# Sorted block attention with a max-out MoE: W2 turned by DMA transposes, and the loads of the later items reordered

## The chip, the cores and the metric

One core of a Trainium2 chip. The metric is the device time of one execution in microseconds; the kernel before takes 166.34 us (median of 3 runs, 166.28 to 167.09). The profile is of one execution with a span of 165.0 us. TensorE multiplies matrices, VectorE (DVE) and ScalarE (ACT) compute on rows and empty PSUM, GpSimd (POOL) issues the loads that cast from float32 to bfloat16, SyncE (SP) issues the stores and DMA transposes.

## The reference

```python
# q, k, v: (4, 8, 768, 64); sort_net: (4, 8, 8, 8); w1, w2: (512, 1024); w_out: (1024, 512)
P = sort_net
for _ in range(5):
    P = exp(P - max(P, -1)); P = P / sum(P, -1); P = P / sum(P, -2)
k_sorted = einsum('bhij,bhjcd->bhicd', P, k_b)     # 8 blocks of 96 rows, mixed by P
v_sorted = einsum('bhij,bhjcd->bhicd', P, v_b)
attn = softmax(q_b @ k_sb^T / 8)                   # within each block
x = (attn @ v_sb) as (3072 tokens, 512)            # heads beside each other
out = maximum(x @ w1, x @ w2) @ w_out              # float32
```

## The kernel before

The batch has four items (b = 0 to 3), each of 8 heads and 768 tokens. For each item the kernel sorts keys and values (a product of the blocks with a block-diagonal matrix made from P), turns queries and keys so that the head dimension lies on partitions, computes scores and their exponentials, the products with the values, a normalisation by a column of ones, and transposes the result x into `xT`. Then comes the MoE for its tokens.

The maximum is rewritten: max(x w1, x w2) w_out = relu(x (w1 - w2)) w_out + x (w2 w_out). So the kernel forms w1 - w2 in place (`w_difference`, in four column quarters; two on GpSimd, two on VectorE, called diff2 and diff3), and once the product wc = w2 w_out (`w_product`, four row blocks). That product needs W2 with its columns on partitions, `w2T`. `w2_transposes` (L634) makes it with TensorE: 16 transposes of 128 x 128 into a PSUM tile, twice, each tile emptied by VectorE or ScalarE. W2 arrives in three column parts, and each group needs the columns up to its own.

The order of all work is written by hand; every engine runs its own instructions in program order. Three pieces set it:

- `front`, a list of names for item 0: k, v (sorts), tq (query transposes), SC (scores), VA (values and normalisation), tx (x transposes), tw (W2 transposes), h..a and h..b (halves of an MoE product of w1 - w2 with xT; h13 is token half 1, column quarter 3), diff, pe2 (block diagonals of the other items), F (512 columns of filler products on TensorE). A last A or D says whether ScalarE or VectorE evacuates.
- For each item b a list of units: 8 `moe_h` (none for b = 0, whose are in `front`), for b = 0 the four `w_product`, then 12 half `moe_out`. So for b = 0 the units 0 to 7 are empty, 8 to 11 are the products for wc, 12 to 23 the outputs.
- `first_tail`, `second_tail`, `third_tail`: the steps of the next item's attention that are put after each unit: KS (key sorts), TQ and `q_transposes`, TURN (`turn_v`, VectorE, which reorders the raw values), VS (value sorts), SC, VA, TR (`x_transposes`, DMA transposes issued by SyncE for items 1 to 3), `pair_q` (copies that set two heads side by side, for the DMA transposes of queries of items 2 and 3).

`evac` (L102) chooses ScalarE or VectorE by a running estimate of their loads (`pick`), unless told. PSUM has four buffers of two banks (`ps_f32`, `ps_bf16`), shared by all products; an unread buffer holds up TensorE.

Loads are issued by GpSimd and wait in its queue, in program order, for the buffer that they overwrite and, when many are in flight, for an older load. The copies into `seen` (L771, L822) are there for order alone: GpSimd waits in them for what they read, and with it the loads behind them. Item 0's values, keys and queries come first, then the parts of W1 and W2, w_out, item 1's keys, item 1's queries, the values of items 1 and 2, item 2's keys and queries (queries of item 2 go into the space of W2, once it is used up). Item 3's values follow in the tail of item 0; its keys and queries go into the space of its own raw values (`load_k`, `load_q`), so they wait until those are turned, in unit 12 of `second_tail`.

Of the kernel before, what the change touches and what calls it, by code (L numbers as in the profile page):

```python
# [11 lines left out]
BF16 = mybir.dt.bfloat16  # L12
# [4 lines left out]
def kernel(  # L17
# [16 lines left out]
    nc = tc.nc  # L34
# [4 lines left out]
    B, H, S, D = q.shape  # L39
# [7 lines left out]
    R = S // 128  # L47
    PB = 128 // NB
    HP = H // 2
# [19 lines left out]
    def ps_bf16(name):  # L69
        return psum.tile([128, 2048], BF16, tag="ps", name=name)  # L70
# [32 lines left out]
    def evac(out_ap, in_ap, n, two_x=False, eng=None):  # L103
        a_ns, d_ns = (200 + n) / 1.2, (130 + (n / 2 if two_x else n)) / 0.96
        if eng:
            load[eng] += a_ns if eng == "A" else d_ns
        if (eng or pick(a_ns, d_ns)) == "A":
            nc.scalar.copy(out=out_ap, in_=in_ap)  # L108
        else:
            nc.vector.tensor_copy(out=out_ap, in_=in_ap)  # L110
# [21 lines left out]
    def load_q(b, by_pair=False):  # L132
        if b == 2:
            t = w2_sb.rearrange("p t f -> p (t f)")[:, 0 : H * R * D].rearrange(
                "p (h x) -> p h x", h=H
            )
        elif b == 3:
            t = v_raw[:, HB * D :].rearrange("p (h x) -> p h x", h=H)
        else:
            t = qpool.tile([128, H, R * D], BF16, tag="q_raw", name="q_raw", bufs=1)  # L140
        src = q[b].rearrange("h (p r) d -> p h (r d)", r=R)
        for hs in [slice(hp, H, HP) for hp in range(HP)] if by_pair else [slice(0, H)]:
            nc.gpsimd.dma_start(out=t[:, hs], in_=src[:, hs])
        q_raw[b] = t
# [5 lines left out]
    NCH = 3  # L150

    def load_k(b):
        k_raw[b] = (
            kpool.tile([128, HB * D], BF16, tag="k_raw", name="k_raw")
            if b < 3
            else v_raw[:, 0 : HB * D]
        )
        n = HB * D // NCH
        for ci in range(NCH):
            nc.gpsimd.dma_start(  # L160
                out=k_raw[b][:, ci * n : (ci + 1) * n],
                in_=k_src[b, :, ci * n : (ci + 1) * n],
            )

    def load_v(b, pieces=2, which=None, half=None):
        r0 = (b % 2 if half is None else half) * 64
        n = BLK * D // pieces
        for m in range(pieces) if which is None else [which]:
            nc.gpsimd.dma_start(  # L169
                out=v_raw[r0 : r0 + 64, m * n : (m + 1) * n],  # L170
                in_=v_src[b, :, m * n : (m + 1) * n],
            )

    w1_sb = big.tile([128, HP, DFF], BF16, tag="w1", name="w1_sb")
    w2_sb = big.tile([128, HP, DFF], BF16, tag="w2", name="w2_sb")
# [10 lines left out]
    def load_w_columns(dst, src, t0, t1):  # L186
        s = src.rearrange("(t p) f -> p t f", p=128)
        c = slice(t0 * DFF // 4, t1 * DFF // 4)
        nc.gpsimd.dma_start(out=dst[:, :, c], in_=s[:, :, c])  # L189
# [208 lines left out]
    nc.vector.memset(v_sb[:, :, D : D + 1], 1.0)  # L398
    xT = big.tile([128, 2, 2, 2, 2, TCH], BF16, tag="xT", name="xT")

    q_pair = {}

    def pair_q(b, two):

# [226 lines left out]
    w2T = big.tile([128, NFB, DMODEL], BF16, tag="w2T", name="w2T")  # L631
    wc = big.tile([128, HP, DMODEL], BF16, tag="wc", name="wc")

    def w2_transposes(t, eng):  # L634
        ps = ps_bf16("tw_ps")
        for n in range(16):
            fb, dmt = t * 4 + n // 4, n % 4
            nc.tensor.matmul(  # L638
                ps[:, n * 128 : (n + 1) * 128],
                w2_sb[:, dmt, fb * 128 : (fb + 1) * 128],  # L640
                ident,
                is_transpose=True,
                start=True,
                stop=True,
            )
        return lambda: evac(
            w2T[:, t * 4 : t * 4 + 4, :].rearrange("p f d -> p (f d)"),
            ps,
            2048,
            two_x=True,  # L650
            eng=eng,
        )

    def w_product(dmt):
# [59 lines left out]
    def moe_out(b, ti, part):  # L714
        slot = ti % 2
        if slot == 0 and part == 0:
            out_ps[0] = ps_f32("out_ps")
        ps = out_ps[0]
        out_products(ps[:, slot * 512 : (slot + 1) * 512], b, ti, part=part)
        if slot == 1 and part == 1:  # L720
            tok0 = b * S + ti * 128
            o = opool.tile([128, 2, 512], FP32, tag="o", name="o")
            evac(o.rearrange("p t n -> p (t n)"), ps, 1024)
            nc.sync.dma_start(
                out=out[tok0 - 128 : tok0 + 128, :].rearrange("(t p) n -> p t n", p=128),
                in_=o,
            )
# [34 lines left out]
    for c, n, m in [(2, 2, 0), (4, 3, 1)]:  # L762
# [4 lines left out]
    turn_v(first, "A", 36, 56)  # L767
    turn_v(first, "A", 56, 80)
    block_diagonals_first()
    seen = const.tile([128, 2, 2], BF16, tag="seen", name="seen")  # L770
    nc.gpsimd.tensor_copy(out=seen[0:G, 0], in_=p_bf[:, NB - 1, NB - 2 :])  # L771
    load_w_columns(w2_sb, moe_w2, 0, 1)
    selections(1)
# [1 line left out]
    turn_v(first, "D", 80, 96)  # L775

    front = """
        k0A k1D k2A v1A v2D v0A tq0D F0 v3D SC1 SC0 tq1D
        SC4 F2 VA1 SC5 F1 VA0 SC3 SC2 VA4 tx0D SC7 F3
        VA3 VA2 SC6 tw0D h00a tx1A tw1A VA5 diff3 diff2 h01a h00bA  # L780
        h01bA tx2A h03a VA6 h03bA VA7 h02a h13a tx3D h02bD h12a h13bA
        pe2 h12bD h10a h11a h10bA h11bA
    """.split()
    fills = [0]

    def fills_due():
# [3 lines left out]
    def front_step(step):  # L790

        eng = step[-1] if step[-1] in "AD" else None
        name = step[:-1] if eng else step
        kind = name.rstrip("0123456789ab")
        n = [int(x) for x in name if x.isdigit()]
        if kind == "F":
            fills[0] = 512
        elif kind == "k":
            sort_k(0, n[0], 640 if step == front[0] else 0, eng)
        elif kind == "v":  # L800
            sort_v(0, n[0], 0, eng)
        elif kind == "tq":
            q_transposes(0, n[0], eng)
        elif kind == "SC":
            scores(0, n[0], fills_due())
        elif kind == "VA":
            values(0, n[0], fills_due())
        elif kind == "tx":
            x_transposes(0, n[0], eng)
        elif kind == "tw":  # L810
            w2_transposes(n[0], eng)()
        elif kind == "diff":
            w_difference(n[0])
        elif kind == "pe":
            block_diagonals([(0, 2), (0, 3), (1, 1), (1, 2), (1, 3)], 2)
        elif name[-1] == "a":
            moe_h_products(0, n[0], n[1], (0, 2), fills_due())
        else:
            moe_h(0, n[0], n[1], eng, (1, 3))

    front_step(front[0])
    nc.gpsimd.tensor_copy(out=seen[:, 1], in_=kT[0][:, 0:2])  # L822
    load_w_columns(w1_sb, moe_w1, 0, 1)
    load_w_columns(w2_sb, moe_w2, 1, 2)
    selections(3)
    load_w_columns(w1_sb, moe_w1, 1, 2)
    load_w_columns(w2_sb, moe_w2, 2, 4)
    load_w_columns(w1_sb, moe_w1, 2, 4)
    load_w(wo_sb, moe_w_out)
    w_difference(0, nc.gpsimd)  # L830
    w_difference(1, nc.gpsimd)
    load_k(1)
    for step in front[1:-26]:
        front_step(step)

    load_q(1)
    for piece in range(2):
        for b in (1, 2):
            load_v(b, which=piece)
    load_k(2)  # L840

    for step in front[-26:]:
        front_step(step)
# [7 lines left out]
    def sorts_and_scores(b):  # L851
# [6 lines left out]
    TURN = [lambda c=c: turn(both, c) for c in (0, 24, 48, 72)]  # L858
    first_tail = {
        7: KS,  # L860
        9: [TQ[0], TURN[0]],
        10: [SC[0], TQ[1], TURN[1]],
        11: SC[1:4] + TURN[2:4] + [lambda half=half: load_v(3, half=half) for half in range(2)],
        12: VS[0:3],
        13: VS[3:6],
        14: VS[6:8] + [SC[4]],
        15: [VA[0], lambda: pair_q(2, 0)],
        16: [VA[1], lambda: pair_q(2, 1)],
        17: SC[5:8] + [TR[0]],
        18: [VA[2]],  # L870
        19: [VA[3], TR[1]],
        20: [VA[4]],
        21: [VA[5], TR[2]],
        22: [VA[6], VA[7], TR[3]],
    }
    SC, VA, TR, KS = sorts_and_scores(2)
    VS = [lambda t=t: sort_v_halved(3, t) for t in range(4)]
    TURN = [lambda c=c: turn(both, c) for c in (0, 24, 48, 72)]
    second_tail = {
        0: [lambda: q_transposes(2, 0), lambda: q_transposes(2, 1)],  # L880
        2: KS,
        4: SC[0:2],
        5: [VA[0]],
        6: SC[2:4] + [TURN[0]],
        7: [VA[1], TR[0]],
        8: [VA[2], TURN[1]],
        9: [VA[3], TR[1], TURN[2]],
        10: SC[4:7],
        11: [VA[4], TURN[3]],
        12: [VA[5], TR[2], lambda: load_k(3), lambda: load_q(3)],  # L890
        13: [VA[6]],
        14: SC[7:8] + VS[0:2],
        15: [VA[7], TR[3]],
        16: VS[2:4],
        17: [lambda: pair_q(3, 0)],
        18: [lambda: pair_q(3, 1)],
    }
    SC, VA, TR, KS = sorts_and_scores(3)
    third_tail = {
        0: [lambda: q_transposes(3, 0), lambda: q_transposes(3, 1)],  # L900
        2: KS,
        5: SC[0:2],
        6: [VA[0]],
        7: [VA[1], TR[0]],
        8: SC[2:5],
        9: [VA[2]],
        10: [VA[3], TR[1]],
        11: [VA[4]],
        12: SC[5:8],
        13: [VA[5], TR[2]],  # L910
        14: [VA[6]],
        16: [VA[7], TR[3]],
    }
    tails = [first_tail, second_tail, third_tail, {}]
    for b in range(B):
# [52 lines left out]
```

The softmax here doesn't subtract the row's maximum and nothing guards it: scores larger than these inputs give would overflow.

## Time and profile before

| | us |
|---|---|
| time, median of 3 | 166.34 |
| span of the profiled execution | 165.0 |
| TensorE busy | 157.0 |
| VectorE busy | 77.5 |
| ScalarE busy | 82.3 |
| GpSimd busy | 33.9 |
| W2 transposes on TensorE | 2 groups of 1.07 |
| their evacuations | DVE 1.21, ACT 1.87 |

The page gives busy time and number of instructions of each engine, the busy share in 40 slices of the span, and the chain of work that ended last: followed back from the last instruction, at each step to what released it, or to the instruction before it on its engine. A timeline row gives start, duration, engine, line, operation, output<-inputs, shapes, how many were merged, and in brackets the idle time before it and what ended it. A load's landing is dated by who was released by it.

### The profile page before, as it was taken

The page shows a single profiled execution, that of the slowest core. Times are in us where ns is not written, and L with a number is a line of the kernel's source. Part 1 is how long each engine was busy: PE and PEld are TensorE (multiplying, and loading weights), DVE is VectorE, ACT ScalarE, POOL GpSimd, SP SyncE. Part 2 cuts the span into 40 slices and gives each one's busy share as a digit, 9 for nine tenths or more (in the row PEclk, how much of TensorE's full clock was granted, in tenths as well). Part 3 has the DMA queues.
Part 4 walks back from the last instruction along what each step waited for, and adds up shares of the span by engine and source line. Part 5 has one row for each costly group of instructions (what it writes and reads, how often), then busy time and mean ns, then how long its engine had stood idle before and what let it go on. Part 6 is the DMA issues. An engine that isn't in the chain of part 4 may idle for free.

```text
span 165.0 us, 4561 instructions
## 1 busy us (share of the span) xinstructions
PE 157.0 (95%) x2007; PEld 95.4 (58%) x2025; DVE 77.5 (47%) x170; ACT 82.3 (50%) x101; POOL 33.9 (21%) x61
## 2 busy tenths in 40 slices
PE   7889999999999999999999999999999999999992
PEld 7839776756554555557655554575655546654451
DVE  4878995684366564525277763250642420000011
ACT  3489776617239846055652353457447206642020
POOL 7949997131206000000014010000000000000000
PEclk9999999999999999999999999999999999999999
DMA  3999999999999999689515999995025294000333
GB/s 41 204 204 194 164 196 207 209 205 220 210 203 204 220 224 167 175 84 228 111 19 104 126 212 157 200 309 29 0 52 175 50 164 142 0 0 0 127 131 127
DMA packets 30404, 23.90 MB, mean 145 GB/s; under 512 B 16752, under 2 KB 25200, under 8 KB 30384
## 3 DMA queue, kind: packets, MB, share of 16 engines
q0 software_dynamic: 11040, 13.37, 50.0%
q1 hardware_dynamic: 19200, 10.17, 28.9%
q8 instruction: 16, 0.26, 0.7%
q10 hardware_dynamic: 144, 0.07, 0.1%
q14 instruction: 4, 0.03, 0.1%
HBM read 26.75 MB, written 6.29 MB: 200 GB/s over the span
## 4 chain that ended last, share of the span: by engine, by line
PE 81%; DMA 6%; DVE 5%; ACT 3%; POOL 2%; issue 2%
PE out_ps L704 37%; PE h_ps L677 25%; DMA w_sb<-in_moe_w_dram 5%; PE wc_ps L657 4%; PE o_ps L575 4%; PE k_ps L458 3%; PE s_ps L548 3%; ACT e L556 1%; POOL w_sb L189 1%; PE v_ps L523 1%; DMA p_sb<-in_sort_net_dram 1%; PE tq_ps L433 1%; DVE colsum L276 1%; DVE p_sb L273 1%; PE tw_ps L638 1%
## 5 line engine op out<-in xcount | busy, mean ns | idle before, releaser
L704 PE MATMUL out_ps<-wo_sb,g 128*128 128x512 bf16 (+2 forms) x187 | 46.0, 370 | 1.4 <-issue 1.0
L677 PE MATMUL h_ps<-xT,w_sb 128*128 128x384 bf16 x256 | 44.5, 326 | 0.0
L677 PEld LDWEIGHTS <-w_sb 128*128 128x128 bf16 x256 | 24.0, 98 | 15.5
L556 ACT ACTIVATE e<-s_ps 96x768 bf16<-96x768 f32 x32 | 24.0, 805 | 14.8 <-PE s_ps L548 14.8
L691 ACT ACTIVATE g<-h_ps 128x768 bf16<-128x768 f32 x27 | 21.7, 811 | 17.4 <-PE h_ps L677 17.3
L704 PEld LDWEIGHTS <-g 128*128 128x128 bf16 x200 | 17.1, 97 | 15.8
L704 PE MATMUL out_ps<-wc,xT 128*128 128x512 bf16 (+2 forms) x98 | 24.7, 370 | 0.1
L108 ACT COPY o<-out_ps 128x1024 f32<-128x1024 f32 x10 | 10.1, 1012 | 28.0 <-PE out_ps L704 25.2
L592 DVE TENSOR_TENSOR x<-o_ps,rs 96x512 bf16<-96x512 f32 x32 | 22.0, 687 | 1.1
L704 PEld LDWEIGHTS <-xT 128*128 128x128 bf16 x100 | 9.6, 97 | 11.2
L575 PEld LDWEIGHTS <-e 96*128 96x128 bf16 x256 | 11.7, 97 | 5.7 <-DVE v_sb L110 0.2
L586 DVE RECIPROCAL rs<-o_ps 96x8 f32<-96x8 f32 x32 | 6.4, 201 | 17.2 <-PE o_ps L575 17.1
L739 DVE COPY o<-out_ps 128x512 f32<-128x512 f32 (+1 forms) x2 | 1.2, 625 | 27.6 <-PE out_ps L704 27.6
L575 PE MATMUL o_ps<-v_sb,e 96*128 96x65 bf16 x256 | 12.7, 193 | 0.0
L110 DVE CAST kT<-k_ps 128x1024 bf16<-128x1024 f32 x6 | 7.2, 1222 | 8.4 <-PE k_ps L458 8.4
L110 DVE CAST v_sb<-v_ps 96x1024 bf16<-96x1024 f32 x7 | 8.5, 1219 | 4.9 <-PE v_ps L523 2.2
L160 POOL DMA_DIRECT2D v_raw<-in_k_dram x3 | 2.5, 838 | 35.1 <-DVE v_dc L250 31.4
L108 ACT CAST v_sb<-v_ps 96x1024 bf16<-96x1024 f32 x9 | 8.8, 1015 | 1.6 <-PE v_ps L500 0.8
L169 POOL DMA_DIRECT2D v_raw<-in_v_dram x11 | 6.5, 593 | 12.7 <-DVE v_dc L250 6.4
L693 DVE TENSOR_SCALAR g<-h_ps 128x768 bf16<-128x768 f32 x5 | 4.8, 957 | 8.9 <-PE h_ps L677 8.8
L548 PEld LDWEIGHTS <-kT 64*128 64x128 bf16 x256 | 6.1, 94 | 4.8 <-issue 2.6
L548 PE MATMUL s_ps<-qT,kT 64*128 64x96 bf16 x256 | 8.5, 204 | 0.3 <-DVE qT L110 0.2
(97 smaller groups left out, 144.4 us busy)
## 6 DMA issues: line engine op xcount, KB each, us to landing
out_dram<-o SPq DMA_DIRECT2D x11, 512.0 KB, 3.4
v_raw<-in_v_dram POOLq DMA_DIRECT2D x8, 384.0 KB, 13.5
k_raw<-in_k_dram POOLq DMA_DIRECT2D x9, 256.0 KB, 11.0
w_sb<-in_moe_w_dram POOLq DMA_DIRECT2D x4, 256.0 KB, 6.0
w_sb<-in_moe_w_dram POOLq DMA_DIRECT2D x2, 512.0 KB, 9.6
wo_sb<-in_moe_w_out_dram POOLq DMA_DIRECT2D x2, 512.0 KB, 13.7
v_raw<-in_v_dram POOLq DMA_DIRECT2D x3, 256.0 KB, 5.0
q_raw<-in_q_dram POOLq DMA_DIRECT2D x4, 192.0 KB, 9.1
```

Source lines behind the costliest of these rows:

```text
L108: nc.scalar.copy(out=out_ap, in_=in_ap)
L110: nc.vector.tensor_copy(out=out_ap, in_=in_ap)
L169: nc.gpsimd.dma_start(out=v_raw[r0 : r0 + 64, m * n : (m + 1) * n], in_=v_src[b, :, m * n : (m + 1) * n],)
L548: nc.tensor.matmul(ps[:, h2 * 512 + ii * 128 : h2 * 512 + ii * 128 + BLK], kT[b][rows, (hp * 8 + i) * BLK : (hp * 8 + i) * BLK + 128], rhs ...
L556: nc.scalar.activation(out=e[:, 0 : 8 * BLK].rearrange("p (t c r) -> p t c r", t=8, r=R), in_=ps[0:BLK] .rearrange("p (t f) -> p t f", t=8 ...
L575: nc.tensor.matmul(ps[:, h2 * 512 + ii * 65 : h2 * 512 + (ii + 1) * 65], e[:, (h2 * 4 + ii) * BLK : (h2 * 4 + ii) * BLK + 128], v_sb[:, m0 ...
L586: nc.vector.reciprocal(out=rs, in_=ov[:, :, :, 64])
L592: nc.vector.tensor_tensor(out=x, in0=ov[:, :, :, 0:D], in1=rs.to_broadcast([BLK, 2, 4, D]), op=ALU.mult,)
L657: nc.tensor.matmul(ps[:, 0:512], w2T[:, fb, dmt * 128 : (dmt + 1) * 128], wo_sb[:, fb, :], start=(fb == 0), stop=(fb == NFB - 1),)
L677: nc.tensor.matmul(h_ps[ch, t][:, m * 512 : m * 512 + TCH], w1_sb[:, hp, fb * 128 : (fb + 1) * 128], xT[:, b % 2, ch, hp % 2, hp // 2, :], ...
L691: nc.scalar.activation(out=g, in_=src, func=AF.Relu)
L704: nc.tensor.matmul(dst, g_tiles[b, ch, m // 2][:, m % 2, off : off + 128] if m < NFB else xT[:, b % 2, ch, hp % 2, hp // 2, off : off + 12 ...
```

## The change

- `w2_transposes` no longer uses TensorE: SyncE issues four DMA transposes, one for each 128 rows of W2, straight into `w2T`. They stand behind all loads of W2. The column loads are reordered, so that the last of W2 is now the last of the six weight parts.
- A third `seen` copy, from the columns of `w2T` that the second transpose writes, stands on GpSimd between item 1's keys and all later loads, so that these start only when that transpose has landed. Item 1's queries are loaded in four parts and the values of items 1 and 2 in eight.
- `front` has a new order: scores, values and h products of item 0 come in another sequence, the W2 transposes are gone, and the fills are added up instead of replaced.
- Item 2's keys are loaded late, in the tail of item 0. Item 3's values are loaded in interleaved halves, its keys and queries get buffers of their own and are loaded right behind its values, after a wait (`hold_loads`) for item 2's query transposes.
- In the tails nearly all steps move: of item 1 the query transposes go from units 9 and 10 to 12 and 13, the turns of the values from 9 to 11 to units 14 and 15, value sorts from 12 to 14 to 17 to 19, x transposes from 17 to 22 to 21 to 23. The tails of items 2 and 3 move by about one unit.
- The output evacuations of item 1 are fixed on ScalarE. The normalisations of the attention stay on VectorE in both kernels.

It is meant to take the transposes and their evacuations off TensorE, VectorE and ScalarE, and to keep later loads out of the way of the DMA transposes.

```diff
@@ load_q, load_k
-        elif b == 3:
-            t = v_raw[:, HB * D :].rearrange("p (h x) -> p h x", h=H)
...
-        k_raw[b] = (
-            kpool.tile([128, HB * D], BF16, tag="k_raw", name="k_raw")
-            if b < 3
-            else v_raw[:, 0 : HB * D]
-        )
+        k_raw[b] = kpool.tile([128, HB * D], BF16, tag="k_raw", name="k_raw")
@@ new
+    seen = const.tile([128, 3, 2], BF16, tag="seen", name="seen")
+    def hold_loads(b):
+        nc.gpsimd.tensor_copy(out=seen[:, 0], in_=qT[b][:, HP - 1, R - 1, 126:128])
@@ w2_transposes
-    def w2_transposes(t, eng):
-        ps = ps_bf16("tw_ps")
-        for n in range(16):
...
-        return lambda: evac(
...
+    def w2_transposes(dmt):
+        nc.sync.dma_start_transpose(
+            out=w2T[:, :, dmt * 128 : (dmt + 1) * 128],
+            in_=w2_sb[:, dmt, :],
         )
@@ moe_out
-            evac(o.rearrange("p t n -> p (t n)"), ps, 1024)
+            evac(o.rearrange("p t n -> p (t n)"), ps, 1024, eng="A" if b == 1 else None)
@@ front
-        k0A k1D k2A v1A v2D v0A tq0D F0 v3D SC1 SC0 tq1D
-        SC4 F2 VA1 SC5 F1 VA0 SC3 SC2 VA4 tx0D SC7 F3
-        VA3 VA2 SC6 tw0D h00a tx1A tw1A VA5 diff3 diff2 h01a h00bA
-        h01bA tx2A h03a VA6 h03bA VA7 h02a h13a tx3D h02bD h12a h13bA
-        pe2 h12bD h10a h11a h10bA h11bA
+        k1A k0A v1D k2A v2A v0D tq0D v3A tq1D SC4 SC5 F2
+        F3 VA4 SC6 SC7 VA5 F0 SC0 VA6 SC1 VA7 F1 SC3
+        tx2D SC2 tx3D VA1 h10a VA0 VA2 h10bA h11a tx0A h11bA diff3
+        VA3 diff2 h13a h01a tx1D h03a h13bD h03bD h01bA h12a pe2 h00a
+        h02a h00bD h02bA h12bA
@@ loads
     load_w_columns(w1_sb, moe_w1, 0, 1)
     load_w_columns(w2_sb, moe_w2, 1, 2)
+    load_w_columns(w1_sb, moe_w1, 1, 2)
+    load_w_columns(w1_sb, moe_w1, 2, 4)
+    load_w_columns(w2_sb, moe_w2, 2, 4)
+    load_w(wo_sb, moe_w_out)
     selections(3)
-    load_w_columns(w1_sb, moe_w1, 1, 2)
-    load_w_columns(w2_sb, moe_w2, 2, 4)
-    load_w_columns(w1_sb, moe_w1, 2, 4)
-    load_w(wo_sb, moe_w_out)
+    for dmt in range(HP):
+        w2_transposes(dmt)
     w_difference(0, nc.gpsimd)
     w_difference(1, nc.gpsimd)
     load_k(1)
+    nc.gpsimd.tensor_copy(out=seen[:, 2], in_=w2T[:, NFB - 1, 254:256])
...
-    load_q(1)
-    for piece in range(2):
+    load_q(1, True)
+    for piece in range(4):
         for b in (1, 2):
-            load_v(b, which=piece)
-    load_k(2)
+            load_v(b, 4, which=piece)
@@ first_tail (item 1)
-        9: [TQ[0], TURN[0]],
-        10: [SC[0], TQ[1], TURN[1]],
-        11: SC[1:4] + TURN[2:4] + [lambda half=half: load_v(3, half=half) for half in range(2)],
-        12: VS[0:3],
...
-        17: SC[5:8] + [TR[0]],
-        18: [VA[2]],
-        19: [VA[3], TR[1]],
-        20: [VA[4]],
-        21: [VA[5], TR[2]],
-        22: [VA[6], VA[7], TR[3]],
+        12: [TQ[0]],
+        13: [SC[0], TQ[1]],
+        14: SC[1:4] + TURN[0:2],
+        15: [SC[4]] + TURN[2:4] + [lambda: load_v(3, half=0), lambda: load_k(2)],
+        16: SC[5:7],
+        17: VS[0:3],
+        18: VS[3:6],
+        19: VS[6:8],
+        20: [VA[0], SC[7], VA[1]],
+        21: [TR[0], VA[2], VA[3], TR[1]],
+        22: [VA[4], VA[5], TR[2]],
+        23: [VA[6], VA[7], TR[3]],
@@ second_tail (item 2)
-        0: [lambda: q_transposes(2, 0), lambda: q_transposes(2, 1)],
+        0: [lambda: pair_q(2, 0), lambda: pair_q(2, 1)],
+        1: [
+            lambda: q_transposes(2, 0),
+            lambda: q_transposes(2, 1),
+            lambda: hold_loads(2),
+            lambda: load_v(3, half=1),
+            lambda: load_q(3),
+            lambda: load_k(3),
+        ],
         2: KS,
...
-        12: [VA[5], TR[2], lambda: load_k(3), lambda: load_q(3)],
```

## The prediction

> **What bounds the kernel now.** I read the page's busy line and slices first, then the chain of waits in order of time, then the timeline of 11 to 52 us, then windows of single stretches.
>
> ```profile
> PE 157.0 (95%) x2007; PEld 95.4 (58%) x2025; DVE 77.5 (47%) x170; ACT 82.3 (50%) x101; POOL 33.9 (21%) x61
> ...
> DMA  3999999999999999689515999995025294000333
> ```
>
> TensorE is busy for 157.0 of 165.0 us, and the transfers are saturated for the first 16 slices, 66 us. So two things run at their limit side by side in the first part of the kernel: whatever leaves TensorE there is worth something only as far as the data are there earlier too. The chain shows where each of them sets the pace:
>
> ```profile
> 16.36 0.67 POOL w_sb L189
> 17.03 8.72 DMA w_sb<-in_moe_w_dram
> 25.75 0.05 issue
> 25.80 1.07 PE tw_ps L638 x16
> ...
> 35.04 3.36 PE h_ps L677 x20
> 38.40 1.64 PE k_ps L458 x96
> 40.03 0.32 PE wc_ps L657
> ```
>
> Until 25.75 the weight loads set the end, and from 25.80 on TensorE itself, without a gap worth a microsecond. The second batch of W2 transposes (tw_ps) stands at the hand-over. The timeline gives the landing times that matter here:
>
> ```profile
> 28.39 1.29 DVE L231 TENSOR_TENSOR w_sb<-w_sb 128x1024 bf16<-128x1024 bf16 x2 [0.32 <-DMA w_sb<-in_moe_w_dram]
> ...
> 34.19 0.52 POOL L169 DMA_DIRECT2D v_raw<-in_v_dram  x1 [1.91 <-DMA wo_sb<-in_moe_w_out_dram]
> ...
> 36.52 0.54 POOL L160 DMA_DIRECT2D k_raw<-in_k_dram  x1 [0.74 <-DMA k_raw<-in_k_dram]
> 37.75 0.53 POOL L160 DMA_DIRECT2D k_raw<-in_k_dram  x1 [0.70 <-DMA k_raw<-in_k_dram]
> 38.33 1.59 PEld L458 LDWEIGHTS <-k_raw 64*64 64x64 bf16 x96 [0.32 <-issue]
> ```
>
> GpSimd's queue waits for an older transfer before it issues a new one, so its releases date the landings: the last weight columns at 28.4, w_out at 34.2, the last third of item 1's keys at 37.7. TensorE sorts those keys from 38.33, only 0.6 us later. The keys have almost no slack.
>
> How loads fare beside DMA transposes is seen in two windows, the first loads alone, the second with x transposes among the key loads of item 3 (columns: window; its length; busy us and instructions of PE, PEld, DVE, ACT, POOL; clock; DMA share; GB/s):
>
> ```profile
> 31.00:35.00 4.00, 4.00 (x41) 2.46 (x38) 2.64 (x5) 0.97 (x2) 1.03 (x2) 1.00 1.15 210
> ...
> 91.00:95.00 4.00, 4.00 (x41) 2.19 (x39) 3.41 (x6) 1.00 (x2) 0.38 (x1) 1.00 1.39 119
> ```
>
> With a higher busy share the engines move little over half as much. That is the resource on which I rest the forecast.
>
> **What the skill says.** "DMA: Bandwidth & Descriptors", section "Queues, rings and completion order": each DMA engine goes round-robin between the queues with work, packet by packet. The packet records agree: beside key loads of 2048-byte pieces, some 90 transpose pieces of 256 bytes and 66 key pieces go out per us, where the keys alone make 94. The same page, "Latency and other measured facts", gives DMA transposes 261 GB/s, so 256 KB would take an estimated 1.0 us; an undisturbed x transpose here moves its 768 pieces in about 1.2 us, which is of that size. "TensorE: Matmul & The Clock Gate", "The HAM clock gate", says that an idle window of about 3.4 us halves TensorE's clock; no stall in this trace is that long (the longest wait is 1.2 us), so it isn't shown here.
>
> **The change part by part.**
>
> *W2 off TensorE.* 32 transposes go: two groups of 1.07 us, 2.14 us. Their two evacuations (DVE 1.21 us, ScalarE 1.87 us) go too; those engines are not the bound there, so I count only the 2.14 us.
>
> *What of it arrives at the key sort.* In the new order the products h13, h01, h03, h12, h00 and h02 stand after the differences diff3 and diff2, which need the last weight columns at 28.4. Both orders queue the same six weight loads, so that time stays. The attention work and h10, h11 before it come to about 14 us of TensorE time from 11.5, plus its small waits: TensorE would be through at 26.3 and stand until diff3 ends at 29.05 (28.4 + 0.65). After that 6 x 1.30 of h, 0.34 of x transposes and 0.25 of block diagonals are left, 8.4 us: the sort of item 1's keys could begin at 37.5 instead of 38.33. So of 2.14 us only 0.8 arrives, and the sort would end at 39.2 rather than 40.03.
>
> *Four DMA transposes beside the loads.* They wait for the last W2 columns, now the last of the six, at 28.4; a transpose starts about 0.9 us after its issue, so 29.3. Each moves 128 x 1024 values, 1024 pieces of 256 bytes. At that time half of w_out (2.4 us alone) and item 1's keys (4 us alone) are still queued on the other ring. Item 3's loads price this: the 256 key pieces from 91 us needed 5.6 us beside one x transpose where they need 2.7 alone (+2.9, some of it to an output store), and the query load from 97 needed 7.5 instead of 4.1; less 0.9 for an output store, +2.5. Both times there was a stretch of 1 to 1.5 us in which nothing finished. About 1000 transpose pieces fall beside w_out and the keys, 1.3 times an x transpose: +3.3 us. The low end is the transpose's own time, +1.2; the high end, with a stall more, +5. I take +3.3: the last third of the keys lands at 41.0, its part of the sort takes 0.55, and the sort ends at 41.6. That is 1.6 us **later** than before. The first product of W2 and w_out waits for the first transpose as well: its 1024 pieces are through at about 40.5 and land about 1 us later, 41.5, the same time by another way. The three others then run alone at 1.0 to 1.4 us each and land ahead of their products (1.9 us each).
>
> *The gate on GpSimd.* The new copy waits for the second transpose, about 43.5 to 44. Behind it on GpSimd's queue stand item 1's queries and the values of items 1 and 2, nothing else. Queries (4.1 us) then land at about 50, values (7.7 us) at about 59. Before, those were 43 and 50. The change has moved their use back: query transposes after units 12 and 13, which is 51 to 54 by the sums above (four products of 1.9, units of 1.3), value sorts after unit 17, about 60.5. The last turn on VectorE ends at about 60. That is hidden with 0.5 us to spare: cost 0, up to 1 us at the high end.
>
> *The seam from item 0's MoE to item 1's.* The second x transpose of item 1 moves from unit 19 to unit 21 of 24. Before, it was held by an output store and its pieces ended at 69.2 for a product that began at 71.1. Now: two value products end 0.5 us after unit 21; VectorE has four normalisations in a row (0.92 each) and ends 2.1 us after it; shortest time to landing 2.8 us, so 4.9. TensorE has units 22 and 23 and six value products until then, 4.1, and two h products (0.32) before it needs that tile: it waits 0.5 us, 1.5 with the usual 3.8 us to landing. I take 0.7.
>
> *The rest.* Item 2's keys loaded late, item 3's values, keys and queries loaded ahead into their own buffers, pair copies (0.55 us each) and query transposes one unit on, item 1's output evacuations on ScalarE: in the windows from 71 to 136 us TensorE is idle for only some 0.9 us, so they can give little; and keys at the sort of item 2 come some 15 us ahead, so they cost nothing. Smaller waits of 0.16 us after value sorts and the like before 71 us may go: -0.4.
>
> Sum: +1.6 (keys late) +0.7 (seam) -0.4 = +1.9; with 0.2 for TensorE running slower after the waits at 26 and 38 us, +2.1: 166.34 + 2.1 = **168.4**.
>
> **The rivals.**
> 1. *Loads late, as summed*: 168.4 (167.2 to 170). For it: the keys' 0.6 us of slack and the 119 GB/s. 0.55.
> 2. *The contention is hidden.* If the transposes cost their own 1.2 us only, or mostly run after the keys, the sort ends at about 39.3 (-0.7); with -0.4 from small waits and the seam at 0 to 0.5, 165.2 to 165.8; I put it at 165.3. For it: the loads after the keys are held back, so the contention is confined to 6 us. Against it: both cases in the trace cost more. 0.32.
> 3. *Waits that feed each other*: the idle stretches at 26 and 38 us halve the clock (some 1.7 us for a window of 3.4), the values land after unit 17 and VectorE, waiting in order on a turn, holds back evacuations: 168.4 + 1.7 + 1 = 171. Against it: the sort's first two thirds break the wait up. 0.13.
>
> **How the numbers follow.** The likeliest case gives 168.4. Below 165.5 (faster by over 0.5%) lies most of the second case, 0.32 with the tail of the first; between 165.5 and 167.2 the edges of the first two, 0.13; the rest slower, 0.55. The range takes the second case's centre at its lower end and the third's at its upper end, 165.2 to 170.8.
>
> **What would show it.** Right: no tw_ps; TensorE waiting for diff3 until about 29; a wait at the key sort on k_raw, ending near 41; the four transposes landing between 41 and 46; a short wait of h_ps on xT at the first seam; nothing new after 75 us. Wrong: keys of item 1 landing before 39, which is the second case; or a long wait at the query transposes or value sorts, which puts the loss in the gate instead.

## The result and the profile after

| | before | after |
|---|---|---|
| time, median us | 166.32 (166.28 to 167.09, 4 runs) | 168.66 (168.10 to 169.27, 4 runs) |
| ratio to before | | 1.0117 (95% interval 1.007 to 1.0164) |
| span of the profiled execution | 165.0 | 166.4 |
| TensorE busy | 157.0 | 156.9 |

The change made the kernel slower by 2.3 us. The page after, the lines that answer to those of before:

```profile
PE 156.9 (94%) x1974; PEld 94.6 (57%) x1993; DVE 73.9 (44%) x168; ACT 81.8 (49%) x101; POOL 37.4 (22%) x70
...
DMA  3999999999999999999599996491025254000333
```

32 transposes fewer, and busy time hardly less: the gain can't be read from this sum, only from the times at which TensorE starts the same work (table below). The saturated stretch of the transfers, 15 slices of 9 before, is now 18 long, then come a 5 and four more 9s. The chain of waits after, in order of time:

```profile
17.07 10.64 DMA w_sb<-in_moe_w_dram
...
27.80 0.70 DVE w_sb L230
28.51 0.05 issue
28.55 1.47 PE h_ps L667 x8
...
33.87 3.36 PE h_ps L667 x20
37.23 1.64 PE k_ps L462 x96
38.86 0.32 PE wc_ps L647
...
62.18 1.93 ACT v_sb L108 x2
64.11 0.04 issue
64.15 0.40 PE o_ps L579 x8
...
68.54 3.75 DMA xT<-x
72.30 0.04 issue
72.34 3.73 PE h_ps L667 x22
```

Two things are to be seen. The sort of item 1's keys (37.23) follows the h products at once: it waits for no keys and comes **earlier** than in the kernel before (38.40). And the chain now leaves TensorE at two places where it did not before, at 62 us for an evacuation of sorted values and at 68.5 us for an x transpose.

The timeline after, rows of TensorE, GpSimd and SyncE, says for how long:

```profile
28.55 1.47 PE L667 MATMUL h_ps<-xT,w_sb 128*128 128x384 bf16 x8 [0.59 <-DVE w_sb L230]
...
64.15 0.40 PE L579 MATMUL o_ps<-v_sb,e 96*128 96x65 bf16 x8 [0.38 <-ACT v_sb L108]
...
71.75 4.32 PE L667 MATMUL h_ps<-xT,w_sb 128*128 128x384 bf16 x24 [1.22 <-DMA xT<-x]
```

```profile
39.18 0.19 POOL L824 COPY seen<-w2T 128x2 bf16<-128x2 bf16 x1 [13.19 <-DMA w2T<-w_sb]
```

```profile
27.80 11.34 SPq L639 DMA_TRANSPOSE w2T<-w_sb  x4
...
66.38 5.17 SPq L609 DMA_TRANSPOSE xT<-x  x3
```

Four W2 transposes keep SyncE's queue for 11.34 us, and GpSimd stands at the gate until 39.2. The profiled execution of the kernel before took 166.83 us, 0.5 above its median; a second trace of it (166.07 us, span 164.2, run c0 below) is the fairer one for places in time. The same two places in its timeline, the sort of item 1's keys and the seam, without a wait:

```profile
37.73 1.71 PE L458 MATMUL k_ps<-bd,k_raw 64*64 64x64 bf16 x96
...
70.34 4.06 PE L677 MATMUL h_ps<-xT,w_sb 128*128 128x384 bf16 x24
```

From here on "before" in tables of places is that second trace; starts of the same TensorE work, in us, and the lag of after:

| TensorE starts | before (c0) | after | lag |
|---|---|---|---|
| sort of item 0's keys | 12.02 | 12.10 | +0.1 |
| sort of item 1's keys | 37.73 | 37.16 | -0.6 |
| first h product of item 1 (seam) | 70.34 | 71.75 | +1.4 |
| sort of item 2's keys | 74.34 | 76.00 | +1.7 |
| last product | 160.94 | 162.82 | +1.9 |

The front gains 0.6 us, the stretch from there to item 2's key sort loses 2.2, and the long rest adds 0.2. The two traced executions lie 2.45 us apart; the last 0.6 of that comes after the last product and outside the span. The front varies by as much as it gains: its key sort stands at 38.33 in the first trace of before, and at 36.75 to 37.23 in the traces of e1, e2 and e6 below, whose front is that of the changed kernel.

### The profile page after: what moved, and what is told of

Its sections match the earlier page's. It is cut to its first block, busy times and chain, and to the rows that moved or that the text cites. A ratio compares the mean times of both kernels' runs of the same rounds, so it can differ in the third digit from the quotient of the medians.

```text
span 166.4 us, 4500 instructions
## 1 busy us (share of the span) xinstructions
PE 156.9 (94%) x1974; PEld 94.6 (57%) x1993; DVE 73.9 (44%) x168; ACT 81.8 (49%) x101; POOL 37.4 (22%) x70
## 4 chain that ended last, share of the span: by engine, by line
PE 79%; DMA 10%; DVE 4%; ACT 2%; POOL 2%; issue 2%; DVEq 0%
PE out_ps L694 36%; PE h_ps L667 24%; DMA w_sb<-in_moe_w_dram 6%; PE wc_ps L647 4%; PE k_ps L462 3%; PE o_ps L579 3%; PE s_ps L552 3%; DMA xT<-x 2%; POOL w_sb L188 2%; PE fill_ps L82 2%; PE v_ps L527 1%; ACT v_sb L108 1%; PE tq_ps L437 1%; DMA p_sb<-in_sort_net_dram 1%; PE v_ps L504 1%
## 5 line engine op out<-in xcount | busy, mean ns | idle before, releaser
L579 PEld LDWEIGHTS <-e 96*128 96x128 bf16 x256 | 11.1, 98 | 6.3 <-ACT e L560 0.7
L729 DVE COPY o<-out_ps 128x512 f32<-128x512 f32 (+1 forms) x2 | 1.2, 625 | 26.3 <-PE out_ps L694 26.3
L108 ACT CAST v_sb<-v_ps 96x1024 bf16<-96x1024 f32 x10 | 9.8, 1009 | 4.9 <-PE v_ps L504 3.4
L171 POOL DMA_DIRECT2D v_raw<-in_v_dram x15 | 8.6, 594 | 8.7 <-DVE v_dc L249 7.1
L110 DVE CAST v_sb<-v_ps 96x1024 bf16<-96x1024 f32 x6 | 7.3, 1220 | 6.5 <-PE v_ps L527 3.2
L110 DVE CAST kT<-k_ps 128x1024 bf16<-128x1024 f32 x5 | 5.9, 1221 | 8.4 <-PE k_ps L462 8.4
L82 PEld LDWEIGHTS <-fill 128*128 128x128 bf16 x98 | 7.9, 129 | 1.7 <-DVE fill L73 1.2
L82 PE MATMUL fill_ps<-fill 128*128 128x118 bf16 x92 | 7.7, 272 | 1.2 <-DVE fill L73 1.2
```

The costliest lines, as they stand in the source:

```text
L82: nc.tensor.matmul(ps[:, 0:w], w0, fill[:, 0:w], start=True, stop=True)
L171: nc.gpsimd.dma_start(out=dst, in_=src)
L579: nc.tensor.matmul(ps[:, h2 * 512 + ii * 65 : h2 * 512 + (ii + 1) * 65], e[:, (h2 * 4 + ii) * BLK : (h2 * 4 + ii) * BLK + 128], v_sb[:, m0 ...
```

## The experiments

"The seam" is the step from item 0's MoE to item 1's. Seam theory: the loss lies in the waits around it, because item 1's attention comes later and its x transposes land later. Rival: the W2 transposes themselves, through the loads, hold up TensorE in the front. The wait at the seam is given below from start to start: what the stretch from the last products before the seam to the key sort of item 2 takes beyond its length without a wait. It is 1.65 us in the changed kernel, of which the timeline row above shows 1.22 as idle. A third question came up on the way: who loses when a DMA transpose and loads meet. The kernel before ran beside each group of runs: 166.20 (e1 to e4), 166.41 (c0, e5 to e7) and 166.15 us (e8 to e10), medians of 11, 11 and 16 runs. Differences of some tenths between versions of different groups are read against these.

**c0, the kernel before again.** 

> The kernel before once more, for a second trace of it: 166.2 within 0.5, the key sort of item 1 at 37.9 to 38.4 us, no wait at the seam.

166.07 us; the key sort at 37.73, just under the stated 37.9, and no wait at the seam. It serves as the trace above.

**e1, item 3's values after the seam.**

```diff
-        15: [SC[4]] + TURN[2:4] + [lambda: load_v(3, half=0), lambda: load_k(2)],
+        15: [SC[4]] + TURN[2:4] + [lambda: load_k(2)],
@@ second_tail, unit 1, behind hold_loads(2)
+            lambda: load_v(3, half=0),
             lambda: load_v(3, half=1),
```

> The changed kernel with one edit: item 3's first half of the values is no longer loaded in the tail of item 0 but behind the wait for item 2's query transposes, so only item 2's keys (0.79 MB) are in flight before the seam from item 0's MoE to item 1's. Seam theory, contention part: the first two x transposes of item 1 (5.2 and 3.75 us to landing in the changed kernel) come down to about 3 us each, the wait of h_ps on xT (1.4 us and 0.27 us) shrinks by about 0.9 us, time about 167.7. If only the place of the steps in the order matters, not the loads beside them: 168.7 as before this edit.

169.33 us (168.54 to 171.71), ratio to before 1.0176 (1.014 to 1.0212): missed. But the step that the edit aimed at came out: from item 1's key sort to item 2's it is 37.88 us instead of 38.84, 0.96 less. The gain is lost before item 3's key sort, 34.59 us on instead of 33.25, at the next seam, where item 2's x transposes now run beside the moved load (timeline of e1, TensorE; the traced execution, 168.54 us, is the fastest of the five):

```profile
104.25 0.49 PE L667 MATMUL h_ps<-xT,w_sb 128*128 128x384 bf16 x2
105.73 0.48 PE L667 MATMUL h_ps<-xT,w_sb 128*128 128x384 bf16 x2 [0.99 <-DMA xT<-x]
```

So in both places the loads beside the x transposes cost about a microsecond.

**e2, item 1 one unit earlier.**

```diff
-        16: SC[5:7],
-        17: VS[0:3],
+        16: SC[5:7] + VS[0:3],
...
-        21: [TR[0], VA[2], VA[3], TR[1]],
+        20: [TR[0], VA[2], VA[3], TR[1]],
```

(and likewise all steps between and behind.) 

> The changed kernel with item 1's value sorts, values and x transposes one unit earlier (units 16 to 22 instead of 17 to 23). Seam theory, order part: the second x transpose is issued one unit (1.3 us of TensorE) earlier relative to the product that needs it, the wait at the seam goes from 1.65 us to about 0.3, time about 167.3. If contention with the late loads sets the landing, the earlier transposes fall deeper into those loads and land no earlier: 168.5. A new wait of up to 0.5 us for the last turn of the values (ends at 55.8 us) is possible at unit 16.

168.42 us (167.77 to 169.18), ratio 1.0131 (1.0099 to 1.0164): the figure of the second alternative, 168.5, and in part its reason. The first two x transposes were issued about a microsecond earlier and landed only half a microsecond earlier (5.77 and 4.08 us after issue instead of 5.24 and 3.75). The wait at the seam is down to 0.7 us; in its place the value sorts wait for turns and evacuations (0.24, 0.16 and 0.29 us of idle time at 55.8 to 57.1).

**e3, W2 by DMA transposes alone, in the kernel before.** The W2 steps are taken out of `front`, the four transposes issued behind w_out; no gate, all else as before.

```diff
-        VA3 VA2 SC6 tw0D h00a tx1A tw1A VA5 diff3 diff2 h01a h00bA
+        VA3 VA2 SC6 h00a tx1A VA5 diff3 diff2 h01a h00bA
...
+    for dmt in range(HP):
+        w2_transposes(dmt)
     w_difference(0, nc.gpsimd)
```

> The kernel before with only W2 turned by DMA transposes (no gate, old order otherwise, transposes issued behind w_out). If the front gain of the changed kernel is that of the transposes: sort of item 1's keys about 0.8 to 1.2 us earlier (37.2 to 37.5), and the seam stays without a wait as in the kernel before, 165.3; but queries and values now share the engines with the transposes, so up to 2 us may come back at the query transposes after unit 9, 166.3 to 167. If the DMA transposes themselves are what costs: 168 or more.

187.89 us (186.88 to 191.81), ratio 1.1304 (1.1267 to 1.1341). Of the alternatives only the open-ended "168 or more" holds it. The trace is of the slowest execution, 191.81 us, so its waits are somewhat long. The waits of TensorE (us in total, times, longest) and SyncE's timeline:

```profile
PE wc_ps L643 <- DMA w2T<-w_sb: 19.1, 2, 11.5
```

```profile
25.66 36.96 SPq L635 DMA_TRANSPOSE w2T<-w_sb  x4
```

The four transposes need 37 us to be issued instead of 11, the slowest lands 29.8 us after its issue. The old order of loads and the missing gate are both in this run; e5 takes them apart.

**e4, the changed kernel with W2 on TensorE.** The groups stand in `front` before tx3 and behind diff2; gate and DMA transposes are out.

```diff
-        tx2D SC2 tx3D VA1 h10a VA0 VA2 h10bA h11a tx0A h11bA diff3
-        VA3 diff2 h13a h01a
+        tx2D SC2 tw0D tx3D VA1 h10a VA0 VA2 h10bA h11a tx0A h11bA diff3
+        VA3 diff2 tw1A h13a h01a
```

> The changed kernel with W2 turned on TensorE again (two groups of 16 in the front, the second right after the last difference; the GpSimd gate on w2T is left out). Seam theory: the front loses what it gained, less what the second group hides of nothing, +1.4 us, and the seam keeps its wait of 1.5 to 2 us: about 169.8. If the DMA transposes and the gate are the cause of the loss: 166.5.

169.47 us (169.35 to 169.52), ratio 1.0192 (1.0161 to 1.0223). Near the figure of the seam theory, 169.8, and the rival's 166.5 is ruled out; but the wait it names is not where it was put. The key sort comes at 39.17, 2.0 us later than in the changed kernel, so the transposes' 2.14 us are worth nearly their whole there; the stretch to item 2's key sort is 38.37 us, 0.5 shorter. The seam costs only 0.7 us there, and TensorE stands for 0.9 us in item 1's value sorts instead, for a reason that the trace doesn't name:

```profile
65.12 0.29 PE L527 MATMUL v_ps<-bd,v_dc 64*128 64x64 bf16 x8 [0.86 <-issue]
```

In this order, then, turning W2 by DMA, with its gate, is worth 0.8 to 0.9 us in all, and the rest of the change, without it, costs 3.3.

**e5, the changed kernel without its gate.**

```diff
-    nc.gpsimd.tensor_copy(out=seen[:, 2], in_=w2T[:, NFB - 1, 254:256])
```

> The changed kernel without the GpSimd gate on w2T, so queries and values are queued while the W2 transposes run. If it is the missing gate that made the transposes in the old order land as late as 67 us: the first lands at about 40, the last after 60, the products for wc wait more than 15 us, 182 or more. If the old order of loads was the cause there: about 170, with the queries 4 us earlier.

182.71 us (181.46 to 183.61), ratio 1.0948 (1.0904 to 1.0993). As expected: it is the missing gate. The transposes as a group, first of the changed kernel (SyncE's rows of the tile w2T):

```profile
L639 SPq DMA_TRANSPOSE w2T<-w_sb x4: 1312/2202/5470, 27.8 to 37.8; - x4
...
DMA to landing us min/median/max: 4.6/8.4/10.5
```

then without the gate:

```profile
L639 SPq DMA_TRANSPOSE w2T<-w_sb x4: 1340/6587/10498, 28.4 to 47.4; - x4
...
DMA to landing us min/median/max: 11.6/16.9/24.9
```

and what TensorE waits for:

```profile
PE wc_ps L647 <- DMA w2T<-w_sb: 11.9, 1, 11.9
```

The loads suffer too: from 41 to 61 us everything together, transposes included, moves 124 GB/s (windows of e5; columns as in the prediction):

```profile
41.00:61.00 20.00, 8.04 (x28) 2.94 (x30) 0.69 (x1) 1.17 (x2) 2.47 (x4) 0.74 1.07 124
```

The 0.74 is TensorE's granted clock. It stayed at 1.00 in the changed kernel from item 0's key sort to the last product; in the long stall of this run it fell to 0.50 from 48 to 58 us, and products of `w_product` took up to 634 ns instead of 379. So a stall of this length costs more than its own time.

What the gate saves is 14 us; what it costs is seen in the changed kernel, from 39 to 41 us, where only the transposes are under way:

```profile
39.00:41.00 2.00, 1.95 (x10) 0.92 (x10) 0.38 (x2) 1.32 (x2) 1.77 (x4) 1.00 1.51 126
```

**e6, item 2's keys early.**

```diff
     load_q(2)
+    load_k(2)
...
-        15: [SC[4]] + TURN[2:4] + [lambda: load_v(3, half=0), lambda: load_k(2)],
+        15: [SC[4]] + TURN[2:4] + [lambda: load_v(3, half=0)],
```

> The changed kernel with item 2's keys loaded right behind item 2's queries, ahead of item 3's values, instead of after them. The load engines have less left beside the first x transposes of item 1. Contention theory: the second x transpose lands about 1 us earlier, the seam's wait drops from 1.65 to about 0.7 and nothing is given back at the next seam, because item 3's values stay where they were: 167.7. Order theory: 168.7.

167.70 us (167.20 to 168.34), ratio 1.0074 (1.0052 to 1.0095): the figure of the contention theory. The second x transpose lands 2.91 us after its issue instead of 3.75. The seam (timeline of e6), a wait of 0.8 us in all:

```profile
70.72 0.48 PE L667 MATMUL h_ps<-xT,w_sb 128*128 128x384 bf16 x2
71.58 3.73 PE L667 MATMUL h_ps<-xT,w_sb 128*128 128x384 bf16 x22 [0.37 <-DMA xT<-x]
```

Nothing comes back later: from item 2's key sort to the last product it is 86.8 us in both. So about 1 of the 2.3 us (1.0 by the medians, 0.8 between the key sorts of the two traces) is the keys of item 2, loaded late and beside item 1's x transposes. The runs of the two kernels overlap slightly (168.10 to 169.27 and 167.20 to 168.34), so this size is not exact.

**e7, and the other waits mended.**

```diff
-        VA3 diff2 h13a h01a tx1D h03a
+        VA3 diff2 h01a h13a tx1D h03a
...
-        16: SC[5:7],
-        17: VS[0:3],
+        16: SC[5:7] + VS[0:2],
+        17: VS[2:5],
...
-        20: [VA[0], SC[7], VA[1]],
+        19: [SC[7], VA[0], VA[1]],
```

(on e6's edit, and all steps between and behind one unit earlier.) 

> As the run before, and item 1's value sorts (two, three, three), values and x transposes one unit earlier, item 1's last scores ahead of its first value product, and in the front the product h01 ahead of h13, so that it fills the wait for diff3. If the loss of the changed kernel lies in these waits (0.54 at the first value product, 1.65 at the seam, 0.6 to 0.76 at diff3): about 165.7, faster than the kernel before by 0.5. If the waits only move elsewhere: 167.5 or more.

167.77 us (167.01 to 167.93), ratio 1.0069 (1.0049 to 1.009): the second alternative. The wait at diff3 is gone (key sort at 36.56), the seam's is down to 0.3 us; a new one stands at the value sorts (timelines of TensorE and VectorE of e7):

```profile
56.72 0.64 PE L527 MATMUL v_ps<-bd,v_dc 64*128 64x64 bf16 x32 [1.32 <-DVE v_dc L249]
```

```profile
55.84 0.82 DVE L249 COPY v_dc<-v_raw 128x768 uint32<-128x768 uint32 x1 [2.12 <-DMA v_raw<-in_v_dram]
```

The last piece of values bounds it. In the kernel before value sorts start at 50.6 with no such wait. In e4, which has neither gate nor DMA transposes, all four turns run without waiting for values, so it is these two that have put the values behind 55.

**e8, the values of items 1 and 2 apart.**

```diff
     for piece in range(4):
-        for b in (1, 2):
-            load_v(b, 4, which=piece)
+        load_v(1, 4, which=piece)
...
     load_q(2)
+    load_k(2)
+    for piece in range(4):
+        load_v(2, 4, which=piece)
...
-    VS = [lambda t=t: sort_v_pair(2, t) for t in range(8)]
+    VS = [lambda t=t: sort_v(1, t) for t in range(4)]
```

(with turns of one half each, item 2's sorts in units 4 and 5 of its tail, item 3's values in halves after them.) 

> A version meant to keep what the W2 transposes give: as the run with item 2's keys early, but item 1's values are loaded and sorted alone (four sorts in units 15 and 16) and item 2's values come after item 2's keys and are sorted in item 2's tail; item 3's upper half of the values follows in the tail of item 0, the lower one in item 1's; h01 ahead of h13. Theory that the values' landing, put back by the time in which the transposes have the engines alone, is what bounds item 1's attention: item 1's values land near 50.5 instead of 55, no wait at the value sorts or the seam, 165.5, faster than before by 0.4 to 0.6%. If the extra 3.3 us of turns on VectorE or the value sorts in item 2's tail bring new waits: 166.5 to 167.5.

174.25 us (173.04 to 176.86), ratio 1.0444 (1.0406 to 1.0482): failed. The trace is of the slowest execution, 176.86 us. Where the edit aimed, only two waits of 0.3 us are left at the value sorts; yet TensorE waits 2.5 us for x transposes at the seam, which land up to 7.5 us after issue, since the loads moved down now meet them, and 1.7 for the turn of item 2's values, which stands on VectorE behind item 2's key evacuations. Here item 1's keys are late too, by 0.8 us at the key sort: the wait that the prediction had expected. The run doesn't show whether a better spread of these loads would do.

**e9, e6 with the two small mends.** e6 with h01 ahead of h13 and SC[7] ahead of VA[0], the sorts left where they are. 

> The run with item 2's keys early (167.7), with h01 ahead of h13 and item 1's last scores ahead of its first value product, the value sorts left in units 17 to 19. If the value sorts have slack there (the last turn ends near 56 us, they start at about 56.7), both small gains come through: 166.9. If the values bound them as in the run with the earlier sorts: 167.7 again.

167.41 us (166.50 to 167.68), ratio 1.0054 (1.0034 to 1.0075); 0.3 less than e6 instead of 0.8, and against the kernel before that ran beside each the same 1.3 us more, so no gain is shown. Both small waits went (key sort at 36.51), but the seam costs 1.1 us again, of which this row shows 0.65:

```profile
70.15 4.31 PE L667 MATMUL h_ps<-xT,w_sb 128*128 128x384 bf16 x24 [0.65 <-DMA xT<-x]
```

Its median is the lowest of the changed kernels here, and it is still slower than the kernel before.

**e10, the last item's part alone, in the kernel before.** Item 3's keys and queries in buffers of their own, issued from unit 1 of `second_tail`, without `hold_loads`.

```diff
         0: [lambda: q_transposes(2, 0), lambda: q_transposes(2, 1)],
+        1: [lambda: load_q(3), lambda: load_k(3)],
...
-        12: [VA[5], TR[2], lambda: load_k(3), lambda: load_q(3)],
+        12: [VA[5], TR[2]],
```

> The kernel before with only the last item's part: item 3's keys and queries in buffers of their own, issued after unit 1 of item 1's MoE instead of after unit 12. Loads there are not waited for in the kernel before (TensorE idle 0.2 us from 104 to 136): 166.3, within 0.4. If they collide with item 2's query transposes or x transposes: a wait at item 2's scores (81 us) or at the seam at 104 us, 167 or more.

174.32 us (173.44 to 175.66), ratio 1.0477 (1.0435 to 1.0519). Neither figure. What I had overlooked: nothing holds these loads on GpSimd's queue once their buffers are their own, so "after unit 1" in the program means nothing. They were issued from 51.9 us, and met item 1's x transposes (SyncE's timeline and TensorE's of e10):

```profile
65.74 9.92 SPq L599 DMA_TRANSPOSE xT<-x  x3
```

```profile
71.58 0.48 PE L671 MATMUL h_ps<-xT,w_sb 128*128 128x384 bf16 x2 [0.94 <-DMA xT<-x]
76.37 2.08 PE L671 MATMUL h_ps<-xT,w_sb 128*128 128x384 bf16 x6 [4.30 <-DMA xT<-x]
```

The four x transposes landed 4.8 to 11.1 us after issue; in the second trace of before, 2.8 to 5.0. The waits come to 5.2 us and the run lost 8.2: after the stall TensorE's granted clock is 0.50 until 82 us (windows of e10):

```profile
78.00:80.00 2.00, 2.00 (x8) 0.95 (x7) 0.00 (x0) 0.81 (x1) 0.00 (x0) 0.50 1.72 168
```

This halving of the clock in a stall, which the prediction cites and had not found in the trace of before, is thus shown by e5 and e10, after stalls of 11.9 and 4.3 us. The changed kernel has no wait that long. In it the loads of item 3's keys and queries stand behind `hold_loads` and are issued from 82.3 us, after the seam; no run takes `hold_loads` out.

## Why the prediction was right in sum and wrong in its largest term

Forecast 168.4 (+2.1), measured 168.66 (+2.3). The sum is right by luck: the largest term, the late keys, did not occur, and others were too small by nearly as much. The prediction had named keys landing before 39 us as the sign that its mechanism is wrong, and they landed at 37.6. By steps, with the lags of the table above:

| step | forecast us | measured us |
|---|---|---|
| weights bound the front, so only part of 2.14 arrives | -0.8 | -0.6 |
| item 1's keys late beside the transposes | +2.4 more, sort +1.6 in all | 0 more |
| gate on GpSimd | 0 (up to 1) | 0 as a wait; bounds what can be mended |
| seam | +0.7 | +1.65 at h, +0.54 before the value products |
| small waits going | -0.4 | 0 |
| slower clock after waits | +0.2 | 0 |
| the rest | 0 | +0.2 to the last product |

**The front** came out near the forecast, but not as worked out. TensorE was to run out of work at 26.3 us and stand 2.7 us for diff3; it ran out at 28.0 us and stood 0.6. What e4 shows is another sum: in the new order the DMA transposes are worth 2.0 us at the key sort, nearly all of the 2.14, and the new order with W2 on TensorE reaches the sort 1.4 us later than the old one does. The weights as a bound were a thin reading too: the wait of 0.38 us before the second group of transposes, on which it rested, is missing in the second trace of before.

**The keys** are where the forecast failed, in the step "About 1000 transpose pieces fall beside w_out and the keys, 1.3 times an x transpose: +3.3 us". The price was taken from loads of item 3 that lost 2.5 to 2.9 us beside one x transpose. Here the last third of the keys landed at 37.6 us, 0.8 later than in the second trace of before and 3.4 earlier than forecast, and the key sort, begun at 37.2, waits for no keys. From 32 to 35 us the load queue (q0) moved 0.54 MB instead of 0.62, before and after (packets, MB, share of the 16 engines):

```profile
q0 software_dynamic: 365, 0.62, 111.7%
```

```profile
q0 software_dynamic: 304, 0.54, 95.7%
q1 hardware_dynamic: 296, 0.08, 18.2%
```

The transposes' queue (q1) finished one piece for each piece of the loads. A piece of a transpose has 256 bytes and one of these loads 2048, so the loads give up about an eighth, and it was the transposes that were put off: four took SyncE 11.34 us, and by the trace's landing marks the first landed 10.5 us after its issue, at 38.3, just ahead of the product that needs it at 38.8. So what I called the second case, at 0.32, is what happened at this point.

This agrees with what the prediction quotes from the Trainium skill ("DMA: Bandwidth & Descriptors", "Queues, rings and completion order"), that each engine goes round-robin between its queues, packet by packet, and it accounts for much of e3 and e5: a transpose of 1024 pieces then goes no faster than the loads beside it finish pieces, and the longer those are, the fewer they are (some 100 per us of 2048 bytes at 33 us of the changed kernel, some 30 of up to 6144 at 45 us of e3). e3 from 32 to 40 us:

```profile
q0 software_dynamic: 903, 1.12, 91.9%
q1 hardware_dynamic: 904, 0.22, 32.1%
```

With no pause in the loads transposes land up to 24.9 us (e5) and 29.8 us (e3) after issue. The 261 GB/s that the prediction quotes for transposes stand on that page for one case, with a non-contiguous middle dimension; from 38 to 39 us of the changed kernel, where nothing ran beside them, they moved 284 GB/s, so their own time was not what was mis-sized. Not everything follows the alternation. At 91 to 94 us of the kernel before 419 pieces of the transposes' queue went by beside 180 of the loads, and from 49 to 58 us of e5 1827 beside 166, at 93 GB/s in all. Why the loads lost so much there and so little here is open: the lengths of their pieces, the output store near them and what else was in flight differ together, and no run took them apart.

**The seam** had the right mechanism, and the sum had it too small: 0.7 against 1.65. The four normalisations in a row and the missing store came out as counted, with the second transpose issued at 68.54. The mis-sized term is the landing: the prediction's own sum gives 0.5 us of wait with its shortest landing, 2.8 us, and 1.5 with 3.8; it took 0.7, and the transpose needed 3.75. It ran beside item 2's keys and item 3's values, which the sum leaves out: in e6, with the keys moved away, it needed 2.91, and the wait fell to 0.8. That these loads "come some 15 us ahead, so they cost nothing" was thought of who waits for the keys, and not of whom the keys hold up. The 0.54 us before the value products, both last evacuations on ScalarE in a row, I had not seen at all.

**The small waits** of 0.16 us were none. They stand before groups of 5 products where the program has 6, with 1.24 us of 1.46 busy: a record is missing there, 0.22 us of work, and the time before the first record looks idle. e2's trace, which has all 48 of these products between the two key sorts, shows none of these waits.

**The gate** cost nothing as a wait, as forecast, and all of it came some 4 us earlier, since the keys were not late: it opened at 39.2 (forecast 43.5 to 44), the last turn ended near 56 us (60), value sorts began at 57.3 (60.5), which leaves 1.5 us to spare. e5 shows that without it 14 us would be lost, and e7 that with it item 1's attention can hardly be moved forward, because the last values land at 55.0, 5 to 7 us later than in the two traces of before.

So the compensation was this: the key sort came 0.6 us earlier where 1.6 later was expected, which is 2.2 less; the seam cost 1.5 more than I had, the small waits gave nothing back (0.4 more), and the clock and the rest cancel. That these nearly balance is chance. What the runs show of the cause: the W2 transposes by themselves gain 0.8 us with the gate (e4); the loss lies after the key sort, around item 1's attention and the seam (the starts in the table); and about 1 us of it comes from the keys of item 2 beside the x transposes (e6). The other 1.3 us is argued from the waits and not shown: e7 and e9 took some of them out, and new ones came or no clear gain, so no version with W2 turned by DMA is faster here than the kernel before.

The larger frame, "whatever leaves TensorE there is worth something only as far as the data are there earlier too", fits what was seen but was not tested by itself: W2's transposes left TensorE, went to the engines that were saturated, and the loads behind them came later.

## What to carry to other kernels

In this kernel the transfer engines were saturated, and there work moved from TensorE to a DMA transpose was not free: it needed a stretch of its own, and the loads behind it came later. A price for contention taken from one place need not hold in another: count the pieces of each queue in the window itself. Keep long loads out of the way of DMA transposes with a wait on the issuing queue, and place that wait by what the queue holds, since a program's line says nothing of when GpSimd issues. And ask of each load that is moved not only who waits for it, but what it will run beside.

## What I had not expected of the hardware

- DMA transposes beside loads finish piece for piece with them: 296 of 256 bytes to 304 of the loads from 32 to 35 us of the changed kernel, 904 to 903 from 32 to 40 us of e3. So the loads lose little there and the transposes much.
- Loads in flight beside DMA transposes stretched a transpose of 256 KB to 20 or 30 us: 4.6 to 10.5 us from issue to landing with the loads behind held back, 11.6 to 24.9 without the gate, up to 29.8 in the old order.
- The same was seen with the smaller x transposes: with item 3's keys and queries beside them (e10) they landed 4.8 to 11.1 us after issue instead of 2.8 to 5.0, and TensorE waited 5.2 us.
- A stall of 4.3 us (e10) was followed by a granted clock of 0.50 up to 82 us, and the run lost 3 us more than the waits.
